# A slot conversion in three steps, a rearranged start, and a token list made by one-hot products, in a fused attention and mixture-of-experts kernel

## Chip, cores and metric

The kernel runs on one core of a Trainium2 chip. The metric is the device time of one execution in microseconds. Before the change it was 625.28 us, the median of 3 runs (625.07 to 625.89).

## The reference

Three stages follow each other. Causal attention over 2 batches, 12 heads, 448 positions and head size 64 gives 896 tokens of 768 values. A dense feed-forward layer (768 to 2048 to 768, with h * sigmoid(1.702 h)) acts on them. A layer of 8 experts (768 to 1024 to 768, ReLU) follows, in which each token goes to one expert.

```
attn = softmax(causal(q @ k.T / 8)) @ v          # f32
x    = attn as 896 tokens x 768
h    = x @ w_in;  x = (h * sigmoid(1.702*h)) @ w_out
e    = argmax(x @ w_gate);  gw = softmax(x @ w_gate)[e]
om   = sigmoid(x @ w_output_gate)[e]
out  = gw * om * (relu(x @ w1[e]) @ w2[e])
```

`w_in` and `w_out` arrive as 64-bit floats, which the chip reads as pairs of 32-bit words; the rest is 32-bit.

## The kernel before

**Precision and conversion.** A large product is made of three products of rounded 32-bit numbers: high by high, high by low, low by high. A tile of 64-bit weights is converted by `work` (L221 to L235). The first step runs two VectorE operations on the words (L226, L228) and then the waiting subtraction of the tile before (`st.flush`, L235). The second step runs a third VectorE operation (L232) and a ScalarE copy of the high part (L234), and puts the subtraction of the low part down as "late". A `yield` separates the two steps. `Stream.pump(n)` (L89) takes n steps, by a credit that may be a fraction, and `need(key)` runs all steps left of a tile at once when a product needs it. There are 48 such tiles: 24 of `w_in`, then 8 and 16 of `w_out`. They live in a ring of 19 slots (three more later); at most 5 raw tiles are loaded ahead.

**Order of the work.** The order of instructions on each engine is written out by hand (`manual_schedule`); each engine runs its own list in order, and waits stand in front of single instructions.

**Attention** runs 12 pairs of heads in 7 steps each (84 steps `s`). A step makes the scores of a block (L374, L375), their maximum on VectorE (L386), the exponential on ScalarE (L388), the normalization (L395 to L397), and four steps later the transposition of the probabilities (L405) and their copy (L408 on VectorE or L410 on ScalarE); the product with V is L423. Steps with s % 7 equal to 3 or 6 end with `st.pump(1)` (24 calls from s = 10 to 90). At the start `load_pair(0)` loads Q and K on SP's queue, eight products of zeros (L459) run on TensorE, and `tr_qk` transposes Q and K (L356), scales Q into two halves of `qz` (L361) and copies K (L365).

**Dense layer 1** runs 16 column blocks `f`; each has six calls of `l1_mm` (36 matmuls, L444), and ends with sigmoid and product in four groups (ScalarE L547, VectorE L548). Each `l1_mm` is followed by one pump step, in the last quarter by two. The accumulators of even and odd `f` lie in different PSUM buffers (3 and 4 of them, two per `f`), so that block f + 2 needs some that block f held.

**Dense layer 2** runs `l2` over 7 token tiles, first 256 columns (part B), then 512 (part A). VectorE and ScalarE split the hidden values (L516, L519) and go on with the conversions, at 0.1 to 0.3 steps per inner index in part B and 1.2 in part A. Between them stand the transposition of the result (`tr_y`, L627) and the router: `logits`, `pick` (chosen expert), `weigh` (its weight), `place`. `place(t)` computes each token's row in the list `xl_d` in DRAM and scatters token number and weight there by an indirect DMA on POOL's queue (L700).

**Experts.** A block (`block`, L880) is 128 tokens of one expert: 12 units of weights, 6 for each of its two products, with hooks at named places: `(hf, k)` inside the first product, 6 to 11 behind a unit of the second. `split` turns a weight unit into high and low parts (ScalarE L307, VectorE L308). Block 0 takes the first 128 tokens of expert 0 found among tiles 0 to 4, while tile 6 is still routed (hooks `last_logits`, `pick`, `last_place`). Block 1 takes the next tokens of expert 0. Its list `le0` is read back from DRAM (`rest_lists` at hook (1, 0), L746); its rows are gathered by `first_x` at hook (1, 3) (L708), and behind them SP waits with a one-element DMA (`gate`, L964) before it goes on loading weights. `prep` at hook 11 transposes the gathered rows (L718) and splits them (ScalarE L720, VectorE L721). In all later blocks `prep` stands at hook 9.

Of the kernel before, what the change touches and what calls it, by code (L numbers as in the profile page):

```python
# [9 lines left out]
F32 = mybir.dt.float32  # L10
# [105 lines left out]
def kernel(ctx, tc, q, k, v, w_in, w_out, w_gate, w_og, w1, w2, out):  # L116
# [49 lines left out]
    with tc.manual_schedule():  # L166
# [1 line left out]
        ident = const.tile([128, 128], F32, name="ident")  # L168
        make_identity(nc, ident)
        identb = const.tile([128, 128], BF16, name="identb")  # L170
        nc.vector.tensor_copy(identb, ident)
        cmask = const.tile([128, QB], BF16, name="cmask")
        for h in range(2):
            make_causal_mask(nc, cmask[QB * h:QB * h + QB], mask_val=NEG)
# [40 lines left out]
        def add64(keys, src, two=False, ring="A"):  # L215
            def load(where):
                raw = raw_tile(where, [128, 512], I64)
                nc.sync.dma_start(raw.rearrange("p (a n) -> p a n", a=2) if two else raw, src)
                return raw

            def work(keys, raw):  # L221
                slot = st.slots[keys[0]] = ring_slot(keys[0])
                r = raw.bitcast(U32).rearrange("p (n two) -> p n two", two=2)
                w = raws.tile([128, 512], F32, name="w32", tag="w32", bufs=2)
                wu = w.bitcast(U32)
                nc.vector.tensor_scalar(wu, r[:, :, 1], 3, 0x3FFFFFF8,  # L226
                                        op0=ALU.logical_shift_left, op1=ALU.bitwise_and)
                nc.vector.scalar_tensor_tensor(wu, r[:, :, 1], 0xC0000000, wu,  # L228
                                               op0=ALU.bitwise_and, op1=ALU.bitwise_or)
                st.flush()  # L230
                yield
                nc.vector.scalar_tensor_tensor(wu, r[:, :, 0], 29, wu,  # L232
                                               op0=ALU.logical_shift_right, op1=ALU.bitwise_or)
                nc.scalar.copy(slot[:, 0], w)  # L234
                st.late = keys[0], lambda: nc.vector.tensor_sub(slot[:, 1], w, slot[:, 0].bitcast(F32))  # L235

            st.add(keys, ring, load, work)
# [82 lines left out]
        NQ = S // QB  # L320
        KC = 128
        NKC = -(-S // KC)
        ld = {}
        qkT = {}
        P_t = {}
# [7 lines left out]
        def load_pair(i):  # L333
            b, hp = pairs[i]
            r = {}
            for nm, src in (("q", q), ("k", k)):
                t = ap_.tile([CP, NB, 2, D], F32, name=nm + "raw", tag=nm + "raw", bufs=2)
                for h in range(2):
                    nc.sync.dma_start(t[:, :, h, :], src[b, 2 * hp + h].rearrange("(c p) d -> p c d", p=CP))
                r[nm] = t  # L340
            ld.setdefault(i, {}).update(r)

# [9 lines left out]
        def tr_qk(i, nm):  # L352
            src = ld[i][nm]
            ps = pa.tile([128, 512], F32, name="ps_tr", tag="tp", bufs=TP)[:, 0:S].rearrange("p (c n) -> p c n", c=NB)
            for c in range(NB):
                nc.tensor.transpose(ps[:, c], src[:, c].rearrange("p h d -> p (h d)"), ident[:CP, :CP])  # L356
            if nm == "q":
                dst = qz[i % 2]
                for h in range(2):
                    r = slice(64 * h, 64 * h + 64)  # L360
                    nc.scalar.mul(dst[r, :, h], ps[r].rearrange("d c p -> d (c p)").rearrange("d (j p) -> d j p", j=NQ),  # L361
                                  0.125)
            else:
                dst = ap_.tile([128, S], F32, name="kT", tag="kT", bufs=2)
                nc.scalar.copy(dst.rearrange("d (c p) -> d c p", c=NB), ps)  # L365
            qkT[i, nm] = dst
# [85 lines left out]
        nc.gpsimd.memset(qz[0], 0.0)  # L452
        load_v(1)
        load_v(2)
        wz = ap_.tile([128, 512], BF16, name="wz")
        nc.vector.memset(wz, 0.0)
        wps = pa.tile([128, 512], F32, name="ps_w", tag="o", bufs=1)
        for i in range(WARM):
            nc.tensor.matmul(wps, wz[:, 0:128], wz, start=True, stop=True)  # L459
# [162 lines left out]
        def tr_y(t, part):  # L622
            n = 4 if part == "A" else 2
            y = ys_t.pop((t, part))
            p = ps.tile([128, 4, 128], F32, name="ps_yT", tag="tp", bufs=2)
            for c in range(n):
                nc.tensor.transpose(p[:, c], y[:, c * 128:(c + 1) * 128], ident)  # L627
            yT = mp.tile([128, 4, 128], F32, name="yT", tag="yT", bufs=1)
            nc.scalar.copy(yT[:, :n], p[:, :n])
            yT_t[t, part] = yT  # L630
# [24 lines left out]
        def pick(t, split_off=False):  # L655
            logits_sum(t)
            lg = lg_t.pop(t)
            nm = mp.tile([128, 8], F32, name="nm", tag="nm", bufs=2)
            tmp = mp.tile([128, 3, NE], F32, name="tmp", tag="tmp", bufs=2)
            ohb = mp.tile([128, NE], BF16, name="ohb", tag="ohb", bufs=2)  # L660
            nc.vector.tensor_reduce(nm[:, 0:1], lg[:, 0:NE], axis=AX.X, op=ALU.max)
            nc.vector.scalar_tensor_tensor(tmp[:, 0], lg[:, 0:NE], nm[:, 0:1], rev,
                                           op0=ALU.is_equal, op1=ALU.mult)
            nc.vector.tensor_reduce(nm[:, 1:2], tmp[:, 0], axis=AX.X, op=ALU.max)
            nc.vector.tensor_scalar(ohb, rev, nm[:, 1:2], None, op0=ALU.is_equal)
            nc.vector.tensor_add(acc[t + 1], acc[t], ohb)
            nc.vector.tensor_scalar(nm[:, 2:3], nm[:, 0:1], -1.0, None, op0=ALU.mult)
            nc.scalar.activation(tmp[:, 1], lg[:, 0:NE], AF.Exp, bias=nm[:, 2:3], scale=1.0,
                                 accum_out=nm[:, 4:5])
            if not split_off:  # L670
                weigh(t, nm, tmp, lg, ohb)
            else:
                late_w.append((t, nm, tmp, lg, ohb))
            ohs[t] = ohb
# [12 lines left out]
        def place(t):  # L687
            ohb = ohs.pop(t)
            p = ps.tile([128, 2 * NE], F32, name="ps_rk", tag="sm", bufs=2)
            nc.tensor.matmul(p[:, 0:NE], sut, ohb, start=True, stop=False)  # L690
            nc.tensor.matmul(p[:, 0:NE], ones, acc[t], start=False, stop=True)
            tmp = mp.tile([128, NE], F32, name="tmp2", tag="tmp2", bufs=2)
            pos = mp.tile([128, 1], F32, name="pos", tag="pos", bufs=2)
            pos_i = mp.tile([128, 1], I32, name="pos_i", tag="pos_i", bufs=2)
            nc.vector.tensor_mul(tmp, p[:, 0:NE], ohb)
            nc.vector.tensor_reduce(pos, tmp, axis=AX.X, op=ALU.add)
            nc.vector.tensor_copy(pos_i, pos)
            while late_w:
                weigh(*late_w.pop())
            nc.gpsimd.indirect_dma_start(  # L700
                out=xl_d[:, :], out_offset=bass.IndirectOffsetOnAxis(ap=pos_i.bitcast(U32), axis=0),
                in_=lst[:, t, :].bitcast(I32), in_offset=None, bounds_check=NT * NE - 1, oob_is_err=False)
# [4 lines left out]
        def gather(lw, xw, nrow=NT):  # L707
            nc.gpsimd.indirect_dma_start(  # L708
                out=xw, out_offset=None, in_=y1_d[0:nrow, :],
                in_offset=bass.IndirectOffsetOnAxis(ap=lw[:, 0:1].bitcast(U32), axis=0),  # L710
                bounds_check=nrow - 1, oob_is_err=False)

        def prep(xw):
            for hf in range(2):
                p = ps.tile([128, 4, 128], F32, name="ps_x", tag="tp", bufs=2)
                for c in range(3):
                    kk = 3 * hf + c
                    nc.tensor.transpose(p[:, c], xw[:, kk * 128:(kk + 1) * 128], ident)  # L718
                dst = xh[:, 3 * hf:3 * hf + 3]
                nc.scalar.copy(dst, p[:, 0:3])  # L720
                nc.vector.tensor_sub(xl[:, 3 * hf:3 * hf + 3], p[:, 0:3], dst.bitcast(F32))  # L721
# [8 lines left out]

        c0_f = mp.tile([128, 1], F32, name="c0_f")
        pos0 = mp.tile([128, 1], F32, name="pos0")
        ix = mp.tile([128, 1 + NOV], I32, name="ix")

        def cut_count():
# [70 lines left out]

        def last_place():
            place(TT - 1)

        def rest_lists():  # L810
            list_at(NOV, le0, NT * (e0 + 1))
# [148 lines left out]
        gate = dram.tile([1, 1], F32, name="gate")  # L960

        def first_x():
            gather(le0, xw)
            nc.sync.dma_start(gate, xw[0:1, 0:1])  # L964

        block(lw0, {
            (0, 1): lambda: tr_y(TT - 1, "A"), (0, 2): last_logits, (0, 3): lambda: pick(TT - 1, True),
            (0, 5): last_place, (1, 0): rest_lists, (1, 3): first_x, (1, 4): counts, 6: further_constants,
            11: lambda: prep(xw)}, (0, 0, 0, 2, 2, 2, 1, 1, 1, 1, 1, 1))
        nov = None  # L970

        def some(p):
# [65 lines left out]
```

## Time and profile before

| | |
|---|---|
| median of 3 runs | 625.28 us |
| the profiled execution | 625.63 us, of it span 623.5 us |
| TensorE (PE) busy | 590.3 us, 95% |
| VectorE (DVE) busy | 463.9 us, 74% |
| ScalarE (ACT) busy | 376.9 us, 60% |
| GpSimd (POOL) busy | 106.7 us, 17% |
| DMA | 118.02 MB, mean 189 GB/s |

Times in the profile count from the span's start. Attention lies at about 0 to 131 us, layer 1 at 121 to 252, layer 2 at 252 to 390, the experts from 389. PEld is TensorE's weight load, which overlaps its matmuls; SPq, ACTq and POOLq are the engines' queues of DMA issues. PEclk is the clock granted to TensorE as a share of full speed. What stands in brackets behind an instruction is how long its engine had been idle, and what ended that.

### The profile page before, as it was taken

What the parts mean: (1) busy time and instruction counts of PE and PEld (TensorE: products, weight loads), DVE (VectorE), ACT (ScalarE), POOL (GpSimd) and SP (SyncE); (2) the same over time, 40 slices, a digit from 0 to 9 for tenths busy, and PEclk for the clock granted to TensorE, in tenths of its full rate; (3) what the DMA queues carried; (4) which work ended last, traced back from release to release, by engine and by line L of the source; (5) the groups of instructions that cost most, each with busy time, mean ns of one, the idle gap of its engine ahead of it and who ended that gap; (6) DMA issues with size and microseconds to landing.
All of it is one profiled execution on the core that took longest, in us unless ns stands there. A gap on an engine that the chain in (4) does not pass through costs nothing. (4 is left out here: it accounts for less than half of the span.)

```text
span 623.5 us, 10060 instructions
## 1 busy us (share of the span) xinstructions
PE 590.3 (95%) x3326; PEld 473.6 (76%) x3326; DVE 463.9 (74%) x942; ACT 376.9 (60%) x743; POOL 106.7 (17%) x225
## 2 busy tenths in 40 slices
PE   7999999899979999889999999989999999999995
PEld 4665665578868888879877777767888888888884
DVE  2788888757858483797633447789998898889886
ACT  4878878623232323455433234678888888888885
POOL 3333333310000000000001002231631111001110
PEclk8999999999979999999999999999999999999998
DMA  5856554216434241433571503359999999999940
GB/s 134 245 125 141 123 126 116 56 57 184 142 111 115 89 136 37 143 116 119 176 263 38 150 17 119 111 183 347 349 368 353 318 383 377 380 381 378 383 161 20
DMA packets 93146, 118.02 MB, mean 189 GB/s; under 512 B 40208, under 2 KB 53408, under 8 KB 93090
## 3 DMA queue, kind: packets, MB, share of 16 engines
q1 hardware_dynamic: 88562, 109.05, 54.7%
q0 software_dynamic: 2512, 5.54, 2.5%
q10 hardware_dynamic: 2016, 2.75, 1.2%
q8 instruction: 28, 0.46, 0.4%
q14 instruction: 28, 0.23, 0.1%
HBM read 114.10 MB, written 7.54 MB: 195 GB/s over the span
## 5 line engine op out<-in xcount | busy, mean ns | idle before, releaser
L587 PE MATMUL py<-slotA,gs 128*128 128x256 f32 (+1 forms) x609 | 112.5, 337 | 1.0 <-DVE gs L519 1.0
L444 PE MATMUL ph<-xhi,slotA 128*128 128x512 f32 (+1 forms) x384 | 97.7, 374 | 5.6 <-DVE g L548 5.6
L587 PEld LDWEIGHTS py<-slotA,gs 128*128 128x128 f32 x609 | 90.8, 190 | 13.6 <-issue 2.6
L444 PEld LDWEIGHTS ph<-xhi,slotA 128*128 128x128 f32 x384 | 70.8, 191 | 16.5 <-issue 6.1
L234 ACT CAST slotA<-w 128x512 fp32r<-128x512 f32 x45 | 27.9, 621 | 63.1 <-DVE w L232 61.4
L308 DVE TENSOR_TENSOR ent<-wraw,ent 128x1024 fp32r<-128x1024 f32 x48 | 57.9, 1221 | 5.8 <-ACT ent L307 5.8
L444 PE MATMUL ph<-xlo,slotA 128*128 128x512 f32 x192 | 56.1, 373 | 0.0
L374 PE MATMUL sc<-kT,qz 128*128 128x64 f32 (+6 forms) x168 | 53.2, 401 | 2.8 <-ACT kT L365 2.4
L388 ACT ACTIVATE P<-sc,nmax 128x64 f32<-128x64 f32 (+6 forms) x84 | 40.3, 479 | 24.5 <-DVE nmax L386 14.7
L548 DVE TENSOR_TENSOR g<-ph,g 128x256 f32<-128x256 f32 x64 | 23.6, 389 | 41.5 <-ACT g L547 41.5
L897 PE MATMUL ps_h<-ent,xh 128*128 128x512 f32 x192 | 54.0, 402 | 0.0
L307 ACT CAST ent<-wraw 128x1024 fp32r<-128x1024 f32 x48 | 49.9, 1053 | 0.0
L519 DVE TENSOR_TENSOR gs<-g,gs 128x512 fp32r<-128x512 f32 x56 | 37.5, 683 | 16.6 <-ACT gs L516 16.6
L397 POOL TENSOR_SCALAR P<-P,rc 128x64 f32<-128x64 f32 (+2 forms) x72 | 36.0, 500 | 69.6 <-DVE rc L396 43.5
L516 ACT CAST gs<-g 128x512 fp32r<-128x512 f32 x56 | 33.8, 618 | 16.3 <-PE py L587 10.6
L386 DVE TENSOR_REDUCE nmax<-sc 128x1 f32<-128x64 f32 (+6 forms) x84 | 34.4, 411 | 10.7 <-PE sc L375 10.7
L547 ACT ACTIVATE g<-ph 128x256 f32<-128x256 f32 x64 | 20.9, 355 | 33.5 <-PE ph L444 17.2
L897 PEld LDWEIGHTS ps_h<-ent,xh 128*128 128x128 f32 x192 | 35.0, 188 | 7.6 <-DVE ent L308 0.3
L308 DVE TENSOR_TENSOR ent<-wrb,ent 128x1024 fp32r<-128x1024 f32 x30 | 36.3, 1223 | 4.7 <-ACT ent L307 4.2
L444 PEld LDWEIGHTS ph<-xlo,slotA 128*128 128x128 f32 x192 | 35.8, 192 | 4.6
L405 PE MATMUL ps_pT<-ident,P 128*128 128x128 f32 x192 | 37.8, 289 | 1.1
L228 DVE SCALAR_TENSOR_TENSOR w<-raw,w 128x512 uint32<-128x512 uint32 x46 | 35.0, 762 | 1.6
(189 smaller groups left out, 1175.5 us busy)
## 6 DMA issues: line engine op xcount, KB each, us to landing
wraw<-in_moe_w_dram SPq DMA_DIRECT2D x66, 512.0 KB
wrb<-in_moe_w_dram SPq DMA_DIRECT2D x48, 512.0 KB
wr<-in_moe_w_dram SPq DMA_DIRECT2D x30, 512.0 KB
raw<-in_moe_w_in_dram SPq DMA_DIRECT2D x24, 512.0 KB
raw<-in_moe_w_out_dram SPq DMA_DIRECT2D x22, 512.0 KB
qraw<-in_q_dram SPq DMA_DIRECT2D x24, 112.0 KB
kraw<-in_k_dram SPq DMA_DIRECT2D x24, 112.0 KB
vraw<-in_v_dram SPq DMA_DIRECT2D x24, 96.0 KB
```

Source lines behind the costliest of these rows:

```text
L228: nc.vector.scalar_tensor_tensor(wu, r[:, :, 1], 0xC0000000, wu, op0=ALU.bitwise_and, op1=ALU.bitwise_or)
L307: nc.scalar.copy(hi, raw)
L308: nc.vector.tensor_sub(lo, raw, hi.bitcast(F32))
L374: nc.tensor.matmul(sc[:, :n], qT[:, j].rearrange("d h p -> d (h p)"), kT[:, :n], start=True, stop=False)
L386: nc.vector.tensor_reduce(nm, sc[:, :n], axis=AX.X, op=ALU.max, negate=True)
L388: nc.scalar.activation(Pb[j][:, :n], sc[:, :n], AF.Exp, bias=nm, scale=1.0, accum_out=sm)
L397: eng[NORM_ENG[j]].tensor_scalar(Pb[j][:, :n], Pb[j][:, :n], rc, 1.0, op0=ALU.mult, op1=ALU.mult)
L405: nc.tensor.transpose(ps[:, c].rearrange("p h q -> p (h q)"), Pb[j][:, c * KC:(c + 1) * KC], ident)
L444: nc.tensor.matmul(p[:, 0:128 * nt], wt, xt[:, kk, 128 * t0:128 * (t0 + nt)], start=kk == 0 and n == 0, stop=kk == KD - 1 and n == 2)
L519: glate.append(lambda: nc.vector.tensor_sub(gs[:, 1], src, gs[:, 0].bitcast(F32)))
L587: nc.tensor.matmul(py[:, :n], gt[:, kk % 4], wt, start=kk == 0 and m == 0, stop=kk == KF - 1 and m == 2)
L897: nc.tensor.matmul(hps[hf], xh[:, k0 + n], wt[:, n], start=k0 + n == 0 and m == 0, stop=False)
```

## The change

Three things change. In `work` a second `yield` follows the ScalarE copy, so that a conversion takes three pump steps, of which the last issues nothing. At the start the zeros for the warm-up are written first, an exponential of one column follows at once, `identb` is copied behind it, pair 0's K is loaded from ScalarE's queue, and the second half of pair 0's scaled Q is written by VectorE. In block 0, `rest_tokens` makes the token numbers of block 1 on the chip: for each of the 7 tiles a 128x128 matrix of 0 and 1 (is this token's place the row wanted?) is multiplied with the token numbers; the gather takes its result `lt0`. `first_x` moves from hook (1, 3) to (1, 1), `rest_lists` from (1, 0) to (1, 2), `prep` from 11 to 9.

```diff
-        nc.vector.tensor_copy(identb, ident)
...
                 nc.scalar.copy(slot[:, 0], w)
+                yield
                 st.late = keys[0], lambda: nc.vector.tensor_sub(slot[:, 1], w, slot[:, 0].bitcast(F32))
...
+        wz = ap_.tile([128, 512], BF16, name="wz")
+        nc.vector.memset(wz, 0.0)
+        ez = ap_.tile([128, 1], F32, name="ez")
+        nc.scalar.activation(ez, wz[:, 0:1], AF.Exp)
+        nc.vector.tensor_copy(identb, ident)
...
+                dma = nc.scalar if i == 0 and nm == "k" else nc.sync
...
+                    if i == 0 and h:
+                        nc.vector.tensor_scalar(dst[r, :, h], src_h, 0.125, None, op0=ALU.mult)
+                    else:
+                        nc.scalar.mul(dst[r, :, h], src_h, 0.125)
...
-            pos = mp.tile([128, 1], F32, name="pos", tag="pos", bufs=2)
+            pos = posn[:, t:t + 1]
...
             nc.vector.tensor_copy(pos_i, pos)
+            if t == TT - 1:
+                rest_hot(t, TT)
...
+        def rest_rows():
+            nc.gpsimd.iota(rowi, pattern=[[1, 128]], base=NT * e0, channel_multiplier=0)
+            nc.vector.tensor_copy(rowc, rowi)
+            nc.vector.tensor_scalar(rowc, rowc, c0_f, None, op0=ALU.add)
+            nc.vector.tensor_copy(tokf, tok_i)
+            nc.vector.tensor_scalar(tokf, tokf, float(-BIG), None, op0=ALU.add)
+
+        def rest_hot(t0, t1):
+            for t in range(t0, t1):
+                nc.vector.tensor_scalar(hot[:, t], rowc, posn[:, t:t + 1], None, op0=ALU.is_equal)
+
+        def rest_tokens():
+            p = ps.tile([128, 2 * NE], F32, name="ps_rt", tag="sm", bufs=2)
+            for t in range(TT):
+                nc.tensor.matmul(p[:, 0:1], hot[:, t], tokf[:, t:t + 1], start=t == 0, stop=t == TT - 1)
+            nc.vector.tensor_scalar(lt0, p[:, 0:1], float(BIG), None, op0=ALU.add)
...
         def first_x():
-            gather(le0, xw)
+            rest_tokens()
+            gather(lt0, xw)
             nc.sync.dma_start(gate, xw[0:1, 0:1])
 
+        rest_rows()
         block(lw0, {
-            (0, 1): lambda: tr_y(TT - 1, "A"), (0, 2): last_logits, (0, 3): lambda: pick(TT - 1, True),
-            (0, 5): last_place, (1, 0): rest_lists, (1, 3): first_x, (1, 4): counts, 6: further_constants,
-            11: lambda: prep(xw)}, (0, 0, 0, 2, 2, 2, 1, 1, 1, 1, 1, 1))
+            (0, 0): lambda: rest_hot(0, 3), (0, 1): lambda: (tr_y(TT - 1, "A"), rest_hot(3, TT - 1)), (0, 2): last_logits, (0, 3): lambda: pick(TT - 1, True),
+            (0, 5): last_place, (1, 1): first_x, (1, 2): rest_lists, (1, 4): counts, 6: further_constants,
+            9: lambda: prep(xw)}, (0, 0, 0, 2, 2, 2, 1, 1, 1, 1, 1, 1))
```

## Rows read from the trace of the kernel before

**Rows 1.** Stages by window: length, busy us of each engine (instructions), PEclk, DMA share, GB/s

```profile
10.00:20.00 10.00, 9.73 (x52) 6.31 (x50) 5.31 (x25) 7.07 (x25) 3.27 (x8) 0.83 0.71 162
60.00:80.00 20.00, 18.98 (x132) 12.24 (x131) 17.47 (x56) 16.23 (x52) 7.49 (x17) 1.00 0.60 135
...
260.00:280.00 20.00, 16.75 (x139) 15.77 (x138) 19.71 (x36) 10.29 (x22) 0.00 (x0) 1.00 0.39 119
...
400.00:410.00 10.00, 8.80 (x48) 7.20 (x48) 9.96 (x12) 8.27 (x10) 5.42 (x23) 1.00 0.09 14
```

**Rows 2.** TensorE's waits, whole span: who waited, for whom, us in total, times, longest

```profile
PE ph L444 <- DVE g L548: 5.6, 2, 5.0
PE ps_o L423 <- DVE pT L408: 3.7, 9, 0.4
PE sc L374 <- ACT kT L365: 2.4, 1, 2.4
...
PE ps_yA L923 <- DVE hl L914: 2.0, 2, 1.2
...
PE ps_h L897 <- ACT xh L720: 1.6, 2, 1.3
```

**Rows 3.** Timeline of the first 10 us: start, duration, engine, instruction

```profile
1.36 0.23 DVE L171 CAST identb<-ident 128x128 bf16<-128x128 f32 x1 [1.36 <-POOL ident masks.py:199]
...
1.72 1.02 SPq L339 DMA_DIRECT2D kraw<-in_k_dram  x2
...
1.92 3.60 PE L459 MATMUL ps_w<-wz 128*128 128x512 bf16 x8 [1.92 <-DVE wz L456]
...
6.34 1.28 ACT L361 ACT_TABLE_LOAD   x1 [6.34 <-PE ps_tr L356]
...
7.64 1.09 ACT L361 ACTIVATE qz<-ps_tr 64x448 f32<-64x448 f32 x2
...
8.75 0.53 ACT L365 COPY kT<-ps_tr 128x448 f32<-128x448 f32 x1
```

**Rows 4.** Timeline of layer 1, one conversion on VectorE and the next one's start

```profile
168.73 0.42 DVE L226 TENSOR_SCALAR w<-raw 128x512 uint32<-128x512 uint32 x1
...
170.40 0.69 DVE L232 SCALAR_TENSOR_TENSOR w<-raw,w 128x512 uint32<-128x512 uint32 x1
...
171.00 0.42 DVE L226 TENSOR_SCALAR w<-raw 128x512 uint32<-128x512 uint32 x1
```

**Rows 5.** Timeline of layer 1's end, two blocks without conversions

```profile
244.57 0.39 ACT L547 ACTIVATE g<-ph 128x256 f32<-128x256 f32 x1 [4.93 <-PE ph L444]
...
246.96 0.29 DVE L548 TENSOR_TENSOR g<-ph,g 128x128 f32<-128x128 f32 x1 [0.34 <-ACT g L547]
...
252.01 0.39 ACT L547 ACTIVATE g<-ph 128x256 f32<-128x256 f32 x1 [4.05 <-PE ph L444]
```

**Rows 6.** The window behind the longest wait in layer 1

```profile
175.70:181.40 5.70, 5.64 (x16) 4.99 (x17) 3.90 (x9) 1.84 (x5) 0.00 (x0) 0.52 0.40 125
```

**Rows 7.** Timeline of layer 2, part B

```profile
277.68 0.44 PE L627 MATMUL ps_yT<-ident,y 128*128 128x128 f32 x2 [1.81 <-ACT y L609]
```

**Rows 8.** Groups by line, whole span: count, busy us, mean ns, idle before

```profile
L650 PEld LDWEIGHTS ps_lg<-esum,lT 128*128 128x128 f32 x14 | 2.6, 188 | 0.9 <-issue 0.4
...
L405 PEld LDWEIGHTS ps_pT<-ident,P 128*128 128x128 f32 x192 | 21.1, 141 | 18.5 <-POOL P L397 14.6 <-POOL rc L395 2.5 <-issue 0.2
...
L397 DVE TENSOR_SCALAR P<-P,rc 128x128 f32<-128x128 f32 x12 | 3.5, 289 | 0.4
```

**Rows 9.** Timeline of block 0 of the experts

```profile
393.06 0.28 DVE L644 TENSOR_TENSOR lT<-ps_lT,lgB 64x128 f32<-64x128 f32 x1 [2.22 <-PE ps_lT L639]
...
406.29 1.87 POOL L708 DMA_INDIRECT xw<-y_d,le  x1 [1.97 <-PE ps_yB L923]
...
407.88 0.73 PE L923 MATMUL ps_yA<-ent,hl 128*128 128x512 f32 x2 [1.20 <-DVE hl L914]
...
413.39 1.19 PE L897 MATMUL ps_h<-entb,xh 128*128 128x512 f32 x4 [1.33 <-ACT xh L720]
```

More of the change, by code (lines that the diff above doesn't have):

```diff
@@ L336, in load_pair @@
             for nm, src in (("q", q), ("k", k)):
+                dma = nc.scalar if i == 0 and nm == "k" else nc.sync
                 t = ap_.tile([CP, NB, 2, D], F32, name=nm + "raw", tag=nm + "raw", bufs=2)
                 for h in range(2):
-                    nc.sync.dma_start(t[:, :, h, :], src[b, 2 * hp + h].rearrange("(c p) d -> p c d", p=CP))
+                    dma.dma_start(t[:, :, h, :], src[b, 2 * hp + h].rearrange("(c p) d -> p c d", p=CP))
                 r[nm] = t
@@ L360, in tr_qk @@
                     r = slice(64 * h, 64 * h + 64)
-                    nc.scalar.mul(dst[r, :, h], ps[r].rearrange("d c p -> d (c p)").rearrange("d (j p) -> d j p", j=NQ),
-                                  0.125)
+                    src_h = ps[r].rearrange("d c p -> d (c p)").rearrange("d (j p) -> d j p", j=NQ)
+                    if i == 0 and h:
+                        nc.vector.tensor_scalar(dst[r, :, h], src_h, 0.125, None, op0=ALU.mult)
+                    else:
+                        nc.scalar.mul(dst[r, :, h], src_h, 0.125)
             else:
@@ L454 @@
         load_v(2)
-        wz = ap_.tile([128, 512], BF16, name="wz")
-        nc.vector.memset(wz, 0.0)
         wps = pa.tile([128, 512], F32, name="ps_w", tag="o", bufs=1)
@@ L732 @@
         pos0 = mp.tile([128, 1], F32, name="pos0")
+        posn = mp.tile([128, TT], F32, name="posn")
         ix = mp.tile([128, 1 + NOV], I32, name="ix")
@@ L808, in last_place @@
             place(TT - 1)
+        rowi = wp.tile([128, 128], I32, name="rowi")
+        rowc = wp.tile([128, 128], F32, name="rowc")
+        tokf = wp.tile([128, TT], F32, name="tokf")
+        hot = wp.tile([128, TT, 128], F32, name="hot")
+        lt0 = wp.tile([128, 1], I32, name="lt0")
+        def rest_rows():
[12 more added lines that the diff above has]
+            nc.vector.tensor_scalar(lt0, p[:, 0:1], float(BIG), None, op0=ALU.add)
         def rest_lists():
```

## The prediction, made before the changed kernel was run

> **What bounds the kernel now.** I read the table of windows first: TensorE is busy in nearly all of each window, at PEclk 1.00, so a gain must come from places where it stands still or is granted less [rows 1]. Then TensorE's waits. The longest is 5.6 us in two waits in layer 1, on VectorE's product L548; then 3.7 us in nine short ones in attention, 2.4 us at the start, and 2.0 and 1.6 us among the experts [rows 2]. Then the timelines around them. The start shows a chain: warm-up, transposes, a table load, two scalings and a copy, one after the other [rows 3]. Layer 1 shows why VectorE was late, below. Two stretches run at half the granted clock (1.2 of 2.4 GHz): 3.4 us of the window from 10 us, as (1 - 0.83) x 10 / 0.5 [rows 1], and 5.5 us behind the 5-us wait, as (1 - 0.52) x 5.7 / 0.5 [rows 6]. The first followed a wait of 2.4 us, the second one of 5.0 [rows 2]; waits of 1.81, 1.20 and 1.33 us [rows 7, 9] left 1.00 in the windows about the first two [rows 1]. TensorE sets the end; I price each part by what it waits less, against the profiled 625.63 us.
>
> **Part 1, conversion in three steps: layer 1.** A conversion takes VectorE 2.27 us from one start to the next, 1.67 of it in the first step [rows 4]. A block f without stalls takes TensorE 7.44 us (252.01 - 244.57), and the chain of sigmoids and products at its end holds VectorE 2.7 us (244.57 to 246.96 + 0.29) [rows 5]. Six pump steps per block are 3 conversions of two steps: 3 x 2.27 + 2.7 = 9.5 us of VectorE against 7.44 of TensorE. It falls 2.1 us behind in each block, until the PSUM buffers are used up and TensorE waits. That goes on for four blocks; then the ring is full and conversions stop. With three steps, 2 conversions per block take 4.5 + 2.7 = 7.2 us, just under 7.44, and the wait never builds up. The step that issues nothing costs nothing. So 5.6 us of waiting go [rows 2], and half of the 5.5 us at half clock, 2.7 [rows 6]: 8.3 us, the largest term.
>
> What is late next: counting the pump calls through, 8 tiles instead of 12 are ready when attention ends, layer 1 then converts two per block up to block 11, and in the last quarter, with 12 steps per block, 4 in block 12 and 3 in block 13. That is 11.8 us of VectorE in block 12 and 9.5 in 13: it falls 4.4 and then 2.1 behind. Block 14 needs only the first two products of 12, which then come 1 to 3 us before it starts; block 13's accumulators are not needed by 14, and 14 converts nothing. I take no stall; if there is one, it is at most what blocks 1 to 4 brought, 8.3. No conversion is forced by `need`: the last ends at the fifth inner index of the first tile of part A, which asks for it at the sixteenth.
>
> **Part 1, layer 2.** In tiles 1 to 3 of part B up to three conversions per tile crowd VectorE (19.71 of 20 us busy, TensorE idle 3.25) [rows 1]; ScalarE waits in line for them and TensorE for ScalarE's copy of the result [rows 7]. At the same fractional pump rates three steps put 3 + 3 + 3 halves of a conversion there instead of 5 + 5 + 4, and spread the rest to later tiles with room. I take 3.0 of these 3.25 us and what lies beside the window; bounds 1.5 and 3.7.
>
> **Part 1, attention.** Four conversions fewer are 4 x 2.27 = 9.1 us less of VectorE. It is busy 17.47 of 20 us there and TensorE 18.98 [rows 1], so this is worth something only where TensorE waits for VectorE: 3.7 us in nine waits [rows 2]. Against it, the cycle of three no longer fits the two pump places of a pair: every third pair has the first step (1.67 us) at s % 7 = 6, where until now only the short second one stood (0.60), ahead of the maxima and copies that the nine waits are on. Gain at most 3; loss at most 3 x (1.67 - 0.60) for the three or four pairs with the long step there, 3.2. I take 0.
>
> **Part 2, the first microseconds.** The memset of zeros stood behind `identb`, which waited for POOL until 1.36, so the warm-up began at 1.92 [rows 3]; put first, it can begin some 0.85 us earlier (estimate; more than 1.36 is excluded). The table load of 1.28 us moves from the chain to the time in which ScalarE had nothing, and one of the two scalings that took 1.09 moves to VectorE, 0.55 [rows 3]. Sum 2.7. But K now stands in ScalarE's list behind the table load and the exponential: its issue of 1.02 us can begin at about 1.1 + 1.28 + 0.2 = 2.6 instead of 1.72 [rows 3], so K lands later by up to 0.9 us while it is needed earlier. I take 2.0 (bounds 0.5 and 2.7). The wait of 2.4 us would shrink below 1, less than any after which the clock fell; of the 3.4 us at half clock at most 1.7 come back, and I take 1.0, since the softmax chain paces part of that time. Together 3.0, bounds 0.5 and 4.4.
>
> The trace shows the activation start at 7.64, right behind the load's end at 7.62 [rows 3]. The Trainium skill (ScalarE: Activation LUTs, What ACT_TABLE_LOAD costs) gives 1283 ns for the load, as here, and 1380 ns of drain beside it; by that the start would gain some 1.4 us more. The row shows no such drain, so the sum leaves it out.
>
> **Part 3, the token list.** Added on TensorE: 7 products with 128x128 f32 weights. Such a product shows as two weight loads (L650: 14 for 7), so 14 loads of 0.141 to 0.188 us: 2.0 to 2.6 [rows 8]. I take 2.1, by the row with the many. Added on VectorE before the last tile's logits: 4 operations in `rest_rows` and 6 comparisons, at most 0.289 each [rows 8], 2.9 us, where VectorE idled 2.22 [rows 9]: the last tile's routing, and TensorE with it, comes 0.7 late (bounds 0, and 1.7 if POOL's iota starts late). VectorE then waits for the product before it goes on splitting weights; there it is full (9.96 of 10 us) [rows 1], and TensorE waited 1.20 us for it [rows 9]. TensorE is pushed by 2.1, VectorE by less, since it idled before its splits; so that wait shrinks, by 0.5 (bounds 0 and 1.2). Moved: `prep` to hook 9. The wait of 1.33 us at the border of blocks 0 and 1 [rows 9], with 0.2 just behind it, goes if the gathered rows are there. They are: the gather was issued at 406.29 [rows 9], and can now be at about 400.5, as soon as the product is done; even 7 us to landing are before hook 9, near 409. The gather goes ahead of `rest_lists` on POOL, whose list is wanted only at block 1's end. SP's gate opens earlier, but the next weights wait for their places, freed by VectorE at about the same time. Sum: + 2.1 + 0.7 - 0.5 - 1.5 = + 0.8, slower (bounds - 0.8 and + 2.8).
>
> **Sum.** - 8.3 - 3.0 + 0 - 3.0 + 0.8 = - 13.5. The profiled execution would take 612.1; it lies 0.35 above the median, so the forecast is 611.8 us.
>
> **Rivals.** (A) *The stall moves to blocks 12 to 15.* For it: 11.8 and 9.5 us of VectorE there. Against it: margins of 1 to 3 us, and the burst ends after two blocks. A full repeat, with the clock, gives back 8.3: 620.1. (B) *K on ScalarE's queue comes too late.* For it: the later issue; two loads in flight share the DMA engines. Against it: K was not waited for before. The start gains 0.5: 614.3. The Trainium skill (DMA: Bandwidth & Descriptors, Issuing engines are not separate DMA queues) says that another issuing engine saves only the sequencer's time; by that, the move brings nothing here, and the trace does not contradict it. (C) *Block 0's chain stretches*: the product waits for the last comparison or the gather is late, a wait passes 2.4 us and the clock falls: + 4 instead of + 0.8: 615. (D) *Slower: attention loses its beat.* The step of 1.67 us delays the maxima in every pair and the delay isn't caught up. It decides from 13.5 / 11 = 1.2 us per pair on; the whole step in each of 11 pairs would be 18.4 us: 630.2. For it: VectorE is 87% busy and in order. Against it: two of three pairs don't have it there. (E) *The conversion count isn't what stalls layer 1*, and only parts 2 and 3 act: 625.28 - 2.2 = 623.1.
>
> **Chances and range.** Forecast 0.69, A 0.10, B 0.08, C 0.07, D 0.03, E 0.03. The forecast's own range is 608.5 to 615; B and C lie within it or at its edge. With 0.2 left outside, 607.5 to 617. Runs differ by about 0.2%, 1.25 us; faster by more than that 0.95, within it 0.02, slower 0.03.
>
> **What would show it.** Layer 1: TensorE idle under 1 us from 126 us to layer 1's end and PEclk 1.00 throughout. Layer 2 part B: under 1.5 us idle. Start: the first score matmul at about 7.3 instead of 9.4, no half clock near 10. Block 0: 14 records of the product, some 2 us; no wait on L720 at the border. I am wrong if layer 1 still waits on L548 for more than 2 us, or if attention's pairs grow longer than before by over 0.3 us each.

## The result and the profile after

The changed kernel takes 616.66 us (median of 4 runs, 616.46 to 617.24), beside it the kernel before 625.58 (4 runs, 625.07 to 625.89): a ratio of 0.986, 95% interval 0.9843 to 0.9877, or 8.9 us less. The forecast was 611.8 with 607.5 to 617.0: the sign and the range hold, the middle is 4.9 too low. The profiled execution took 616.5 us, span 614.2.

Stages, in us, read from timelines of both kernels (first score matmul; ScalarE's copies of attention's pairs and of layer 2's tiles; POOL's scatters of the blocks' results). The last column is the prediction's term.

| stretch | before | after | change | forecast |
|---|---|---|---|---|
| start to the end of pair 1 | 25.35 | 22.55 | -2.80 | -3.0 |
| pairs 2 to 12 | 104.49 | 103.58 | -0.91 | 0 |
| layer 1, to layer 2's first matmul | 122.15 | 119.74 | -2.41 | -8.3 |
| layer 2, part B | 50.43 | 46.27 | -4.16 | -3.0 |
| layer 2, part A | 87.58 | 88.32 | +0.74 | 0 |
| block 0 to block 1's scatter | 44.26 | 42.83 | -1.43 | +0.8 |
| from there to the last scatter | 182.46 | 184.19 | +1.73 | 0 |
| sum | | | -9.24 | -13.5 |

TensorE's waits after (what it waited for: us in all, times, the longest), beside [rows 2]:

```profile
PE ph L453 <- DVE g L555: 4.1, 1, 4.1
PE ps_pT L414 <- POOL P L406: 3.2, 5, 0.9
PE ps_tr L362 <- DMA kraw<-in_k_dram: 1.6, 2, 1.2
...
PE ps_yA L957 <- DVE hl L948: 1.2, 2, 0.7
...
PE ps_o L432 <- DVE pT L417: 1.2, 3, 0.4
PE py L594 <- DVE gs L526: 1.0, 1, 1.0
...
PE ps_h L931 <- ACT xh L729: 0.2, 1, 0.2
```

The wait on the product of layer 1 is still the longest: 4.1 us once, for 5.6 in two. Of the nine waits on attention's copies three are left (1.2 us for 3.7), but five on POOL are new, and so are two on the loads of K. At the border of blocks 0 and 1 only 0.2 of the 1.6 us for `xh` is left.

Windows of after, beside [rows 1] (engines' busy us and counts, then PEclk, DMA share, GB/s):

```profile
10.00:20.00 10.00, 9.27 (x60) 5.88 (x58) 6.81 (x29) 8.04 (x28) 4.15 (x10) 1.00 0.90 229
60.00:80.00 20.00, 19.04 (x134) 12.42 (x134) 16.41 (x56) 15.52 (x49) 7.22 (x17) 1.00 0.47 105
220.00:240.00 20.00, 15.87 (x71) 13.69 (x70) 16.50 (x32) 6.51 (x14) 0.00 (x0) 0.91 0.43 131
260.00:280.00 20.00, 19.44 (x164) 18.18 (x163) 18.03 (x33) 11.19 (x24) 0.00 (x0) 1.00 0.31 100
```

In attention VectorE's load fell from 17.47 to 16.41 us of 20; in layer 2's crowded window TensorE now stands 0.56 us instead of 3.25. The window from 220 us is new: 4.13 idle, and PEclk 0.91, which is (1 - 0.91) x 20 / 0.5 = 3.6 us at half clock, or 1.8 lost.

Timeline around it, all engines, with the first product (L555) of blocks 0 and 10 ahead of it:

```profile
130.36 0.42 DVE L555 TENSOR_TENSOR g<-ph,g 128x256 f32<-128x256 f32 x1 [3.04 <-ACT g L554]
...
208.20 0.42 DVE L555 TENSOR_TENSOR g<-ph,g 128x256 f32<-128x256 f32 x1 [1.02 <-ACT g L554]
...
214.32 0.68 DVE L231 SCALAR_TENSOR_TENSOR w<-raw,w 128x512 uint32<-128x512 uint32 x1
...
215.09 0.62 ACT L233 CAST slotA<-w 128x512 fp32r<-128x512 f32 x1 [1.65 <-DVE w L231]
...
215.62 0.38 ACT L554 ACTIVATE g<-ph 128x256 f32<-128x256 f32 x1
...
216.03 0.42 DVE L555 TENSOR_TENSOR g<-ph,g 128x256 f32<-128x256 f32 x1 [1.03 <-ACT g L554]
...
218.21 0.42 DVE L225 TENSOR_SCALAR w<-raw 128x512 uint32<-128x512 uint32 x1
...
225.01 0.42 DVE L225 TENSOR_SCALAR w<-raw 128x512 uint32<-128x512 uint32 x1
...
228.39 0.42 DVE L555 TENSOR_TENSOR g<-ph,g 128x256 f32<-128x256 f32 x1 [1.02 <-ACT g L554]
...
229.83 0.66 PE L453 MATMUL ph<-xhi,slotA 128*128 128x384 f32 x1 [4.13 <-DVE g L555]
```

Block 11's product starts at 216.03, block 12's at 228.39. Between 218.21 and the last start at 225.01 lie four conversions, 2.27 apart. Block 14 wants the accumulators of 12 from 225.7 on and gets them at 229.83.

The rows also show a cost that the forecast left out. VectorE ends its step at 215.00; then ScalarE must copy that tile (215.09) before it comes to block 11's sigmoid (215.62), and VectorE stands for 1.03 us. A block with two conversions so takes VectorE 7.83 us (216.03 less the product of block 10 at 208.20), not 7.2, against TensorE's 7.44. From block 0's product at 130.36 on, eleven blocks take 85.67 us, 7.79 each.

The start after, beside [rows 3]:

```profile
0.75 1.28 ACT L326 ACT_TABLE_LOAD   x1 [0.75 <-PEq L1058]
...
1.18 0.96 ACTq L345 DMA_DIRECT2D kraw<-in_k_dram  x2
...
5.56 0.58 PE L362 MATMUL ps_tr<-ident,kraw 112*128 112x112 f32 x4 [0.41 <-DMA kraw<-in_k_dram]
...
6.18 0.53 ACT L374 COPY kT<-ps_tr 128x448 f32<-128x448 f32 x1 [0.39 <-PE ps_tr L362]
...
6.76 0.43 PE L383 MATMUL sc<-kT,qz 128*128 128x64 f32 x2 [0.62 <-ACT kT L374]
```

K's issue did not wait for the load and the exponential, as the prediction had it: it ran at 1.18, during the load. The first score matmul came 2.67 us earlier.

Block 0 after, beside [rows 8, 9]:

```profile
382.28 1.26 DVE L836 TENSOR_SCALAR hot<-rowc,posn 128x128 f32<-128x128 f32 x6
...
383.51 0.28 DVE L651 TENSOR_TENSOR lT<-ps_lT,lgB 64x128 f32<-64x128 f32 x1
...
387.35 1.76 PEld L841 LDWEIGHTS ps_rt<-tokf,hot 128*128 128x128 f32 x14
...
389.70 1.76 POOL L717 DMA_INDIRECT xw<-y_d,lt  x1 [0.30 <-DVE lt L842]
...
398.89 0.73 PE L957 MATMUL ps_yA<-ent,hl 128*128 128x512 f32 x2 [0.66 <-DVE hl L948]
...
402.96 0.86 PE L931 MATMUL ps_h<-entb,xh 128*128 128x512 f32 x3
```

The 14 weight loads take 1.76 us, the wait on `hl` falls from 1.20 to 0.66, and block 1 starts at 402.96 without a wait.

### The profile page after: what moved, and what is told of

Read it like the earlier page. It is cut to its first block, busy times and chain, and to the rows that moved or that the text cites. A ratio compares the mean times of both kernels' runs of the same rounds, so it can differ in the third digit from the quotient of the medians.

```text
span 614.2 us, 10097 instructions
## 1 busy us (share of the span) xinstructions
PE 588.6 (96%) x3340; PEld 472.9 (77%) x3340; DVE 464.6 (76%) x955; ACT 377.7 (61%) x743; POOL 107.0 (17%) x226
## 5 line engine op out<-in xcount | busy, mean ns | idle before, releaser
L383 PE MATMUL sc<-kT,qz 128*128 128x64 f32 (+6 forms) x168 | 51.6, 390 | 1.0 <-ACT kT L374 0.6
L555 DVE TENSOR_TENSOR g<-ph,g 128x256 f32<-128x256 f32 x64 | 23.6, 389 | 30.5 <-ACT g L554 30.5
L414 PEld LDWEIGHTS ps_pT<-ident,P 128*128 128x128 f32 x192 | 21.1, 141 | 21.7 <-POOL P L406 18.0
L227 DVE SCALAR_TENSOR_TENSOR w<-raw,w 128x512 uint32<-128x512 uint32 x46 | 33.1, 720 | 1.6
```

Source lines behind the costliest of these rows:

```text
L383: nc.tensor.matmul(sc[:, :n], qT[:, j].rearrange("d h p -> d (h p)"), kT[:, :n], start=True, stop=False)
L414: nc.tensor.transpose(ps[:, c].rearrange("p h q -> p (h q)"), Pb[j][:, c * KC:(c + 1) * KC], ident)
```

## The experiments

**The three parts, each alone on the kernel before.** The first is the second `yield` (`x1_steps`), the second the rearranged start (`x2_start`), the third the token list with the moved hooks (`x3_list`).

> The kernel before with the second yield alone. Theory (the steps empty VectorE's line in layer 1 up to block 11, and the four conversions in block 12 build one new stall): first matmul of layer 2 at 251.99 - 2.4 - 0.9 = 248.7, one wait of 3 to 5 us on the product of block 12 and nothing longer than 1 us in blocks 1 to 11; layer 2 3.4 us shorter; time 625.6 - 6.7 = 618.9. Rival (the stall in block 14 comes from the shifted start of the changed kernel, not from the steps): no wait over 1 us in layer 1, half clock nowhere, layer 1 8.3 shorter: 613.5. Rival (the steps cost something in attention that the earlier start hid): pairs 0.3 us longer each, time above 621. The product of the experts' blocks stays at 18.23 us per block in each of these.

> The kernel before with the rearranged first microseconds alone. Theory: first score matmul at 6.8 instead of 9.4, no half clock in the window from 10 us, pair 1 ends 2.8 us earlier and every later pair too; layer 1 keeps its waits of 5 us on the product and its half clock, as its VectorE work is unchanged; layer 2 and the blocks as before: 625.6 - 2.8 = 622.8. Rival (VectorE's line in attention and layer 1 takes the time back): the first pair gains 2.8, the first matmul of layer 2 less than 1: 624.8.

> The kernel before with the one-hot token list and its earlier transposes alone (a tile posn of 28 bytes takes the place of two of 4, and what is allocated behind lies 32 bytes lower). Theory (the place of gs, hh and hl in SBUF sets the rate of the products that take them as weights): start, attention and layer 1 as before, tiles of layer 2 part A 12.52 us apart instead of 12.42, block 0 0.9 shorter, blocks 1 to 8 18.40 instead of 18.23: 625.6 + 1.0 - 0.9 + 1.4 = 627.1. Rival (the slower blocks come from the gap-free layer 1 and layer 2 ahead of them): blocks 18.23, time 624.7.

| run | time | ratio to before, 95% |
|---|---|---|
| x1_steps | 619.32 (618.76 to 621.04) | 0.9893, 0.9877 to 0.991 |
| x2_start | 623.11 (622.53 to 623.96) | 0.9954, 0.9937 to 0.997 |
| x3_list | 626.22 (625.29 to 627.56) | 1.0009, 0.9999 to 1.0019 |

With 625.60 beside them that is -6.28, -2.49 and +0.62, together -8.15 of the -8.92 of all three; the times lie within 1 us of the expected 618.9, 622.8 and 627.1. The steps alone leave the same wait in layer 1, so the stall in block 14 isn't the start's. First TensorE's waits in `x1_steps`, then its windows, then the window of `x2_start`:

```profile
PE ph L445 <- DVE g L549: 4.5, 1, 4.5
```

```profile
10.00:20.00 10.00, 9.74 (x51) 6.47 (x49) 4.62 (x19) 6.20 (x21) 2.85 (x7) 1.00 0.63 140
220.00:240.00 20.00, 15.50 (x63) 13.32 (x62) 17.09 (x34) 5.90 (x14) 0.00 (x0) 0.83 0.50 158
```

```profile
10.00:20.00 10.00, 9.91 (x51) 7.01 (x50) 5.27 (x23) 7.15 (x23) 3.39 (x8) 0.74 0.72 183
```

Here my expectation of `x2_start` missed: its clock fell to half near 10 us after waits of at most 1.2 us. `x1_steps`, with the old start and its wait of 2.4 us, reads 1.00 in that window, but its products there take nearly twice as long, as at half clock: its trace has no clock record before 14.71 us, and the window counts that as 1.00. The same two products of 320 columns, first in the kernel before, at full clock, then in `x1_steps`:

```profile
9.70 0.78 PE L374 MATMUL sc<-kT,qz 128*128 128x320 f32 x2
```

```profile
9.95 1.42 PE L375 MATMUL sc<-kT,qz 128*128 128x320 f32 x2
```

So all three executions with the old start ran at half clock behind that wait (`x3_list` reads 0.88 in the window from 10 us), and four of the eleven with the new start fell near 10 us. The new start does not rule the half clock out; that it makes it rarer is likely, but not shown by so few executions. What the half clock costs there is close to the 1.0 us that I took: with the new start pair 1 ends at 22.1 to 22.9 us without it, and at 23.2 to 23.6 where it lasted 3.4 us. The Trainium skill (TensorE: Matmul & The Clock Gate, What's actually happening) says that the cost of getting up to speed varies from run to run with one and the same kernel; these traces agree: the four transposes of the first K take 0.58 us in the changed kernel and 0.98 in `x10_kqueue`, with the same start but for K's queue (both rows are shown).

The list alone brings tiles of part A 12.50 to 12.54 us apart (12.40 to 12.44 before) and blocks 18.38 to 18.43 (18.22 to 18.23), with layer 1 and part B as before. So the slower blocks come with the list, and not from a layer 1 without gaps.

**Where tiles lie in SBUF.** The list's `posn` takes the place of two small tiles. By the kernel's memory allocation all that is allocated behind moves down 32 bytes: `gs` (the tile that layer 2's products load as weights), `hs`, and `hh` and `hl` (the weights of the experts' second products). `hh` and `hl` came to lie on a multiple of 128 bytes (32 above one before), `gs` 64 above one (96 before). Three kernels put unused bytes back:

```diff
+            mp.tile([128, 8], F32, name="padp", ...)      # x4_pad32; 16 columns in x7_pad64
             pos = posn[:, t:t + 1]
...
+        wp.tile([128, 8], F32, name="padw")               # x8_padw alone
         hh = wp.tile([128, KF2, 128], F32R, name="hh")
```

> The changed kernel with an unused tile of 32 bytes where the tile pos stood, so that gs, hs, hh and hl lie where they lay before. Theory (their place sets the rate): tiles of layer 2 part A 12.42 apart, blocks 18.23, products on hh of 256 columns 278 ns instead of 282, all else as in the changed kernel: 616.7 - 2.2 = 614.5. Rival (the slower products come from somewhere else in the change): 12.52, 18.40 and 616.7.

> The changed kernel with an unused tile of 64 bytes instead of 32: gs, hs, hh and hl lie 64 bytes higher than in the changed kernel, 32 higher than before. Theory (an address that is a multiple of 64 bytes is the slow one, 32 above it the fast): as the changed kernel, tiles of part A 12.52 apart, blocks 18.40. Rival (any shift from the changed kernel's place brings the speed back, or only multiples of 128 are slow): 12.42 and 18.23, or hh (now 64 above a multiple of 128) fast and gs (now on a multiple of 128) slow: 12.52 with 18.23.

> The changed kernel with 32 unused bytes between hs and hh: hh and hl lie where they lay before, gs and hs stay in the changed kernel's place. Theory (it is the place of the tile that the product loads as weights): blocks 18.23, tiles of part A still 12.52. Rival (the place of hs, which is transposed and written out, counts, or the total volume behind): blocks 18.38 to 18.43.

| kernel | `gs` above a multiple of 128 | tile of part A | `hh`, `hl` above a multiple of 128 | block |
|---|---|---|---|---|
| before | 96 | 12.40 to 12.44 | 32 | 18.22 to 18.23 |
| after | 64 | 12.50 to 12.54 | 0 | 18.38 to 18.43 |
| x4_pad32 | 96 | 12.39 to 12.43 | 32 | 18.18 to 18.23 |
| x7_pad64 | 0 | 12.53 to 12.56 | 64 | 18.31 to 18.32 |
| x8_padw | 64 | 12.50 to 12.54 | 32 | 18.18 to 18.25 |

The products on `hh` in all five, from 470 to 580 us (durations in ns: min/median/max), in the table's order:

```profile
L921 PE MATMUL ps_yB<-ent,hh x96: 276/278/280, 481.8 to 578.6; 128*128 128x256 f32 x96
L921 PE MATMUL ps_yA<-ent,hh x48: 387/393/476, 483.2 to 577.1; 128*128 128x512 f32 x48
```

```profile
L955 PE MATMUL ps_yB<-ent,hh x96: 278/282/286, 471.2 to 569.0; 128*128 128x256 f32 x96
...
L955 PE MATMUL ps_yA<-ent,hh x48: 392/396/482, 472.7 to 567.5; 128*128 128x512 f32 x48
```

```profile
L956 PE MATMUL ps_yB<-ent,hh x96: 276/276/280, 472.2 to 569.0; 128*128 128x256 f32 x96
...
L956 PE MATMUL ps_yA<-ent,hh x48: 387/393/476, 473.6 to 567.5; 128*128 128x512 f32 x48
```

```profile
L956 PE MATMUL ps_yB<-ent,hh x96: 277/280/282, 471.1 to 568.3; 128*128 128x256 f32 x96
...
L956 PE MATMUL ps_yA<-ent,hh x48: 392/397/476, 472.5 to 566.8; 128*128 128x512 f32 x48
```

```profile
L956 PE MATMUL ps_yB<-ent,hh x96: 276/276/283, 471.2 to 567.9; 128*128 128x256 f32 x96
...
L956 PE MATMUL ps_yA<-ent,hh x48: 387/393/480, 472.6 to 566.4; 128*128 128x512 f32 x48
```

All data is the same, and TensorE's clock is 1.00 throughout. With `hh` 32 bytes above a multiple of 128 the products take 276 to 278 and 393 ns, with it on one 282 and 396, and 64 above it 280 and 397. In `x8_padw` `hs` and `gs` stayed where the changed kernel has them, the blocks got their speed back and part A did not: each follows the place of the tile that its product loads as weights. My expectation for `x7_pad64` (18.40) missed by 0.09: the place 64 above is slow, but less so. What in the read of the weights is slower was not measured.

`x4_pad32` takes 615.59 us (614.23 to 616.07; 0.983 of before, 0.9813 to 0.9846). Its part A and its blocks behind block 1 are 0.78 and 1.72 us shorter than the changed kernel's, together 2.5; its median is only 1.1 lower. The profiled execution had half clock at the start and 6.8 us of it in layer 1 instead of 3.6, so I take the stages for the price. The whole times do not tell the places apart: single runs of `x7_pad64` and `x8_padw` took 615.49 and 614.76 us.

**The stall in layer 1.** One line, on top of the 32 bytes:

```diff
-    R1, R1B = 1, 2
+    R1, R1B = 1, 1                       # x5_pump1
+    R1, R1B = 0.95, 0.95                 # x6_pump95; x9_even also evens R2
```

> The changed kernel with the 32 unused bytes and with one pump step per product in layer 1's last quarter instead of two (2 conversions in each of blocks 12, 13, 14 instead of 4, 3, 0). Theory (the burst in block 12 makes the stall): VectorE's blocks stay 7.8 us apart, the product of block 12 comes some 4.5 us earlier than with the burst, TensorE waits for it under 1 us, no half clock behind it; layer 2 gets one conversion more, at most 1 us: 615.6 - 4.1 - 1.8 to 3.4 + 0.5 = 609 to 610.5. Rival (VectorE's 7.8 us per block against TensorE's 7.44 have used up the lead by block 12, with or without a burst): a wait of 2 us or more in block 14 or 15 and half clock behind it: 613 or more.

> As the run with one step per product in the last quarter, but 0.95 step per product in all of layer 1: block 7 converts one tile instead of two, and layer 2's first tile of part A four instead of three. Theory: VectorE regains 2.3 us at block 7, so that no wait on the product over 0.3 us is left in layer 1, and the tile of part A has room: 0.3 to 0.8 us below the run with one step. Rival (the extra conversion costs layer 2 what layer 1 saves): the same time within 0.5 us.

> As the run with 0.95 step per product in layer 1, but with layer 2's part B pumping more evenly (0.15, 0.3, 0.25, 0.3, 0.3, 0.3, 0.3 steps per inner index instead of 0.1, 0.3, 0.3, 0.3, 0.15, 0.3, 0.2), so that three conversions instead of four are left for the first tile of part A. Theory (TensorE's waits on slotA in that tile are the fourth conversion's price): no wait on slotA, first tile of part A 11.0 to 12.4 us instead of 15.51, layer 2 part B at most 1 us longer: 613.8 - 2.5 = 611.3, and below the run with one step per product (612.2). Rival (the added steps crowd the tiles of part B as they did in the kernel before): part B 2 us or more longer and 613 to 614.

> The changed kernel with the 32 unused bytes, 0.97 pump step per product in all of layer 1 (one conversion instead of two in block 11, two in each of 12 to 14) and 0.2 instead of 0.1 in layer 2's first tile, which leaves three conversions for the first tile of part A. Theory (the wait on gs at the start of layer 2 is VectorE's lag of one conversion in block 14, and four conversions in the tile of part A are one too many): no wait on the product in layer 1, under 0.5 us at the start of layer 2 and no half clock there, first tile of part A at most 12.4 us, part B at most 1.5 longer than its best: 609 to 610.5. Rival (each conversion taken out of layer 1 costs layer 2 as much): 612 to 614, with 2 us or more of waits in part B or in the tile of part A.

> The run with one pump step per product in the last quarter again, beside the one with 0.97: 612.2, with its wait of 1.7 us on gs and the half clock behind it at the start of layer 2. If that wait comes with 1 us or less, or no half clock follows, the stretch at the start of layer 2 is a matter of the single execution, and the two kernels differ by less than the theory says.

| run | time | ratio to before, 95% | layer 1 | part B | first tile of part A | layers 1 and 2 |
|---|---|---|---|---|---|---|
| x4_pad32 | 615.59 | 0.983, 0.9813 to 0.9846 | 120.78 | 46.68 | 11.79 | 255.0 |
| x5_pump1 | 612.17 | 0.979, 0.9771 to 0.9808 | 115.86 | 49.71 | 11.00 | 252.3 |
| x12_pump1_again | 612.18 | 0.9779, 0.9761 to 0.9797 | 115.86 | 49.73 | 11.08 | 252.4 |
| x11_pump97 | 613.26 | 0.9803, 0.9784 to 0.9821 | 114.06 | 49.57 | 13.06 | 252.5 |
| x6_pump95 | 613.78 | 0.982, 0.9796 to 0.9844 | 114.05 | 47.42 | 15.51 | 252.8 |
| x9_even | 614.81 | 0.9825, 0.98 to 0.9849 | 114.05 | 52.60 | 11.45 | 254.1 |

The burst was the cause: with two conversions per block in the last quarter no wait on the product is left, and layer 1 is 4.9 us shorter. But 612.2 isn't the expected 609 to 610.5. Windows of `x5_pump1`, then the next wait of its TensorE:

```profile
220.00:240.00 20.00, 20.00 (x98) 17.43 (x96) 14.89 (x30) 6.69 (x16) 0.00 (x0) 1.00 0.51 158
240.00:260.00 20.00, 18.12 (x136) 17.44 (x136) 16.73 (x32) 11.48 (x26) 0.74 (x1) 0.91 0.35 118
```

```profile
241.80 0.50 PE L594 MATMUL py<-slotA,gs 128*128 128x256 f32 x2 [1.65 <-ACT gs L523]
```

VectorE's lag of 0.35 us per block (7.79 against 7.44) is now paid at the border: block 14's chain ends late, `gs` behind it too, and 3.6 us at half clock follow a wait of 1.65, in both runs of this kernel. Waits of 1.0 at the same place, in the kernels before and after, left 1.00. But the length of a wait does not decide alone: one of 1.89 us in layer 2 of `x3_list` was followed by half clock (0.97 and 0.95 in the windows from 260 and 280 us), while waits of 1.81 us at the same place in the kernel before and in `x2_start`, and one of 2.47 us in `x9_even` (shown below), left 1.00.

With one conversion fewer in layer 1 this wait is gone and layer 1 takes 114.05, but the conversion turns up in layer 2. First `x6_pump95`, in the first tile of part A, then `x9_even`, at the end of part B:

```profile
299.99 0.49 PE L594 MATMUL py<-slotA,gs 128*128 128x512 f32 x1 [1.11 <-ACT slotA L233]
301.01 0.73 PE L594 MATMUL py<-slotA,gs 128*128 128x512 f32 x2 [0.52 <-DVE slotA L235]
302.26 0.49 PE L594 MATMUL py<-slotA,gs 128*128 128x512 f32 x1 [0.52 <-ACT slotA L233]
```

```profile
294.20 0.44 PE L634 MATMUL ps_yT<-ident,y 128*128 128x128 f32 x2 [2.47 <-ACT y L616]
```

So by the last column (252.5 to 254.1 against 252.3 and 252.4) the rival in these three expectations holds: a conversion taken out of layer 1 costs layer 2 as much or more, wherever it is put. The whole times of `x6_pump95` and `x9_even` are even 1.1 and 0.8 us above the rival's; the profiled executions of both ran at half clock near 10 us. The version with one step per product and the 32 bytes beats both kernels, with 612.2 us in two runs, 4.5 below the changed kernel (0.979 and 0.978 of the kernel before, against 0.986).

**K's queue.** Back to SP (`x10_kqueue`, one run, 615.26 us):

```diff
-                dma = nc.scalar if i == 0 and nm == "k" else nc.sync
+                dma = nc.sync
```

> The changed kernel with the 32 unused bytes, and the first pair's K issued from SP behind Q, as in the kernel before, instead of from ScalarE. Theory (the issue at 1.18 on ScalarE, beside the table load, is 0.5 us earlier than at 1.72 on SP, and K lands as much earlier): k transposes wait for K 0.5 us longer, first score matmul at 7.3 to 7.5 instead of 6.8 to 7.0. Rival (the queue makes no difference, as both copies share the DMA engines with Q): first score matmul at 6.7 to 7.0.

```profile
1.73 1.02 SPq L345 DMA_DIRECT2D kraw<-in_k_dram  x2
...
5.61 0.98 PE L362 MATMUL ps_tr<-ident,kraw 112*128 112x112 f32 x4
...
7.21 0.43 PE L383 MATMUL sc<-kT,qz 128*128 128x64 f32 x2 [0.62 <-ACT kT L374]
```

The issue is 0.55 us later, yet K's transposes don't wait for it: they start at 5.61, and in the changed kernel at 5.56, behind a wait of 0.41 for K. So for an issue 0.55 us later K was there at most 0.05 us later in these two executions. The first score matmul at 7.21 lies between the two expectations, because K's transposes took 0.98 us and not 0.58; the other ten executions with the new start reach from 6.60 to 7.10. A gain by K's queue is not to be seen.

## Why the prediction was right, and where it was off

**Layer 1, -8.3 forecast, -2.4 measured: the step that failed** is the one on blocks 12 to 15: "Block 14 needs only the first two products of 12, which then come 1 to 3 us before it starts [...] I take no stall". They came 4.1 us after. The counts of 2, 4 and 3 conversions were right. The time of a block was not: 7.2 was the sum of two conversions and a chain measured where no conversion ran [rows 5], which leaves out that ScalarE's copy stands ahead of the sigmoid in its own list. 7.79 instead puts VectorE 0.35 behind in each of eleven blocks, 3.8 us in all, before the burst begins. That is rival A at 0.10, though with one wait instead of two and 5.9 us given back instead of 8.3; `x5_pump1` shows that the burst triggers it. The first half of the reasoning held: blocks 1 to 11 run without a wait and at 1.00.

**The slower late blocks and part A, 0 forecast, +2.5 measured.** No step looked at where tiles lie. `x4_pad32` and `x8_padw` show that this is the cause.

**Block 0, +0.8 forecast, -1.4 measured.** The product was 1.76 us (2.1 forecast), the wait on `hl` 0.54 shorter (0.5), the border's 1.5 gone (1.5). Wrong was the 0.7 for late routing: six of the seven comparisons take 0.21 us each instead of 0.289, and `lT` at 383.51 held nobody up. TensorE is busy only 0.9 us more in blocks 0 and 1 (41.61 for 40.70) and idle 2.3 less; why 0.9 and not the product's 1.76 was not followed up.

**Layer 2's part B, -3.0 forecast, -4.2 measured**: the direction is right, the size 0.5 past its larger bound. **Attention, 0 forecast, -0.9 measured**: every third pair, the one with the long step at s % 7 = 6, takes 9.88 instead of 9.46, as feared, but the other two take 9.0. **The start, -3.0 forecast, -2.8 measured**: close by luck, since its parts were off. The first score matmul came 2.67 earlier (2.0 forecast), since the issue of K didn't wait. From there to the end of pair 1 TensorE is busy 13.85 us instead of 15.56, at a granted clock of 1.00 instead of 0.89, so 1.7 came back by the clock of these two executions (1.0 forecast). Most of that went into a wait that no step had, for the next pair's K:

```profile
9.09 0.57 PE L362 MATMUL ps_tr<-ident,kraw 112*128 112x112 f32 x4 [1.21 <-DMA kraw<-in_k_dram]
```

All eleven executions with the new start show this wait, of 0.5 to 1.2 us; none with the old start does. Why that K comes late was not tested.

## What to carry over

Counting an engine's work per iteration isn't enough where two engines hand work back and forth: measure the period of that loop in a stretch that has all of it, and multiply the difference to the bounding engine by the number of iterations. Work that is only moved to fit (a conversion here) comes due at the next border; look for the border before counting the gain. And when a change adds or drops a small tile, compare the durations of products that the change doesn't touch: here 32 bytes cost 1% of every block. Check a granted clock, too, against the durations of like products before building on it.

## What the hardware showed unexpectedly

A product whose 128x128 f32 weights lie on a multiple of 64 bytes takes 2 to 6 ns longer than with the tile 32 bytes above one (256 columns: 280 and 282 ns against 276 to 278; 512 columns: 396 and 397 against 393): 18.41 us per block of experts against 18.23, 12.52 per tile against 12.42. A DMA issue on ScalarE's queue ran at 1.18 us while that engine loaded a table (0.75 to 2.03). Near 10 us the half clock came in some executions and not in others of the same start; behind a wait of over 4 us in layer 1 it came each time, behind one of 1.65 both times, and behind one of 2.47 in layer 2 it did not.
